# Root as a power on GpSimd, a group's sums ahead of its scores, another rule for the spare PSUM tile, and a split output tail in an attention + MLP kernel

## The chip, the cores and the metric

The kernel runs on one core of a Trainium2 chip. The metric is device time in microseconds (us), as the median of several runs. The engines are named as in the profile: PE (TensorE, matrix products), PEld (its weight loads), ACT (ScalarE), DVE (VectorE), POOL (GpSimd) and SP (SyncE, which here only issues DMAs). A q behind a name means the engine's instruction queue. [...]

## The reference

Attention with normalised queries and keys, then an MLP with a leaky rectifier:

```
batch, heads, seq, dim = 8, 12, 448, 64
q_n = q / sqrt(mean(q*q, -1) + 1e-6) * g_q           # the same for k with g_k
attn = softmax(q_n @ k_n.T / 8)                       # per batch and head
x = (attn @ v) as [8*448 tokens, 12*64]
h = x @ w_in                                          # 768 -> 2048
out = (max(h, 0) + alpha * min(h, 0)) @ w_out         # 2048 -> 768, fp32
```

All inputs and the output are fp32. Inside, the products take fp16.

## The kernel before, in words

**Tiling.** A batch has three groups of four heads, so there are 24 groups, numbered y = 3*batch + i. Partitions 0 to 63 hold two heads of the group, partitions 64 to 127 the other two. The 448 positions are cut into J = 7 tiles of 64.

**Preparing a group.** `load_qk(y)` brings q and k (tile `nat`, four DMAs), on SP, or half on ACT's queue for the first two groups. `square` makes the squares (ACT for y < 2, POOL after), `reduce` sums them on DVE (`ss`), `root` turns the 28 sums of a partition into 1/sqrt(mean + eps) (`rr`) with two ACT instructions, Ln and then Exp with scale -0.5 (L152, L153), and `scale` multiplies q and k by it (`qs`, L158), mostly on POOL. For y < 8, `turn` transposes q and k on PE (L193) into PSUM, and DVE copies them out, k with the gain g_q*g_k; later groups are transposed by DMA on SP (`turn_dma`), and `turn` is then only the product of k and gain on DVE (L179).

**Attention.** `score(y, j)` makes the transposed scores of one 64-key tile for four heads (four matmuls into the two-bank tile `sc`, of which there are two), and `soft` the exponential on ACT (L227) into `expT`. When all seven tiles of a group are there, `den(y)` sums them over the keys by 28 matmuls with ones, `log` and `invert` make the reciprocal on ACT (Ln, then Exp with scale -1, L253, L258), and `attv(y)` multiplies by v (28 matmuls), scaled by DVE into `xT` (L266). `den`, `attv` and the transposes of groups 3 to 7 share a single two-bank PSUM tile with the tag `acc`.

**MLP.** `up(b, ft)` makes 128 of the 2048 hidden columns for one batch: six matmuls (L281), an ACT copy times alpha (`ah`, L289), a DVE maximum (`gT`, L290) that frees the bank. `down(b0, t, oh)` makes 128 tokens by 384 columns of the output from a pair of batches: 16 matmuls (L298), a DVE copy (`osb`, L310), and after the second half two DMAs of 64 rows (L314). Both write to one of two single-bank PSUM tiles (tag `mm`), or, when `spare` is given, to the `acc` tile (`bank`, L271), where the trace calls them hTa and opa.

**Order.** The order on every engine is the order of the code; nothing reorders it. The attention is cut into 66 slots n of two or three score tiles (`bursts`). `dens` and `avs` say in which slot each group's `den` and `attv` stand, alternately; `turn_at`, `roots`, `prep` (before a slot), `post` (after it) and `jobs` (behind the matmuls of a `down`) say where the preparations of later groups stand. A planner deals the MLP units to the slots (`gaps`) by estimated costs, UP = 1.13, DOWN = 2.6 and a cost per slot, so that each batch's units are spread over the 15 slots or so that follow its last `attv`. A slot runs: `prep`, the first two scores and their exponentials, `den` or `attv`, the third score and its exponential, `log` and `invert`, `root` and `scale` of a later group, then the MLP units with `turn` behind the first one. The units of the last batch follow all slots (`rest`). Slots without units at the start hold dummy matmuls (`spin`) that keep PE running. In each slot without a PE transpose, the unit with number k == 2 takes the spare tile:

```
            spare = k == 2 and not turns.get(n, TD) < TD
```

The four loads of `w_in` stand together before slot 0 on POOL's queue, those of `w_out` before slots 10 to 13.

Of the kernel before, what the change touches and what calls it, by code (L numbers as in the profile page):

```python
# [9 lines left out]
FP32 = mybir.dt.float32  # L10
# [11 lines left out]
def kernel(  # L22
# [46 lines left out]
    nc.vector.memset(expb, EXP_BIAS)  # L69
    epsb = cst.tile([128, 1], FP32, name="epsb", tag="epsb")  # L70
    nc.vector.memset(epsb, RMS_EPS)
    ones = cst.tile([128, 64], FP16, name="ones", tag="ones")
    nc.vector.memset(ones, 1.0)
    ident = cst.tile([128, 128], FP16, name="ident", tag="ident")
# [40 lines left out]
    def load_w_in(c):  # L115
        nc.gpsimd.dma_start(
            out=w_in_sb[:, :, ts(c, FB)],
            in_=moe_w_in[:, ts(c, FB)].rearrange("(k p) f -> p k f", p=128),
        )
# [18 lines left out]
    def reduce(y, nm):  # L138
        if nm == "q":
            ss_t[y] = ld.tile([128, 2, 2, J], FP32, name="ss", tag="ss", bufs=4)  # L140
        nc.vector.tensor_reduce(  # L141
            out=ss_t[y][:, "qk".index(nm)].rearrange("p h j -> p (h j)").unsqueeze(2),
            in_=sqs[y, nm], axis=AXIS_X, op=ALU.add,
        )

    def root(y, nms="qk"):
        n = len(nms)
        at = "qk".index(nms[0])
        if at == 0:
            rr_t[y] = ld.tile([128, 2, 2, J], FP32, name="rr", tag="rr", bufs=4)  # L150
        rr, ss = rr_t[y][:, ds(at, n)], ss_t[y][:, ds(at, n)]
        nc.scalar.activation(out=rr, in_=ss, func=AF.Ln, scale=1.0 / D, bias=epsb[:, 0:1])  # L152
        nc.scalar.activation(out=rr, in_=rr, func=AF.Exp, scale=-0.5)  # L153

    def scale(y, nm):
        t = ld.tile([128, J, 2, D], FP16, name="qs", tag="qs", bufs=4)
        eng = nc.vector if (y, nm) in ((0, "k"), (1, "q"), (1, "k")) else nc.gpsimd
        eng.tensor_mul(  # L158
            out=t.rearrange("p j h d -> p h j d"),
            in0=nat[y, nm],  # L160
            in1=rr_t[y][:, "qk".index(nm)].unsqueeze(3).broadcast_to((128, 2, J, D)),
        )
        qs[y, nm] = t
# [11 lines left out]
    def turn(y):  # L175

        if y >= TD:
            t = qkT[y, "k"].rearrange("p j g c -> p (j g c)")
            nc.vector.tensor_scalar(  # L179
                out=t, in0=t, scalar1=gain[:, 0:1], scalar2=None, op0=ALU.mult  # L180
            )
            return
        if y < G:
            ps = [psf.tile([128, 512], FP32, name="tps", tag="mm") for _ in "qk"]
        else:
            ps2 = psa.tile([128, 2, 512], FP32, name="tps2", tag="acc")
            ps = [ps2[:, 0], ps2[:, 1]]
        tps = [
            t[:, : S].bitcast(FP16).rearrange("p (j c) -> p j c", j=J) for t in ps
        ]  # L190
        for tp, nm in zip(tps, "qk"):
            for j in range(J):
                nc.tensor.transpose(  # L193
                    tp[:, j, :], qs[y, nm][:, j].rearrange("p h d -> p (h d)"), ident
                )
        for tp, nm in zip(tps, "qk"):
            t = att.tile([128, J, 2, 64], FP16, name=f"{nm}T", tag=f"{nm}T", bufs=4)
            o = t.rearrange("p j g c -> p j (g c)")
            if nm == "q":
                nc.vector.tensor_copy(out=o, in_=tp)  # L200
            else:
                nc.vector.tensor_scalar(  # L202
                    out=o, in0=tp, scalar1=gain[:, 0:1], scalar2=None, op0=ALU.mult
                )
            qkT[y, nm] = t
# [41 lines left out]
    def den(y):  # L247
        dn = over_keys("dn", y, lambda g, par, j: ones[ds(64 * g, 64), :])
        rden[y] = dn
# [27 lines left out]
    def up(b, ft, spare=False):  # L277
        x = xT[b].rearrange("p g i c -> p (g i) c")
        hT = bank("hT", spare)
        for c in range(KM):  # L280
            nc.tensor.matmul(  # L281
                out=hT[:, :S],
                lhsT=w_in_sb[:, c, ts(ft, 128)],
                rhs=x[:, c, :],
                start=(c == 0),
                stop=(c == KM - 1),
            )
        ah = ffn.tile([128, S], FP16, name="ah", tag="ah", bufs=3)
        nc.scalar.activation(out=ah, in_=hT[:, :S], func=AF.Copy, scale=alpha_sb[:, ft : ft + 1])  # L289
        nc.vector.tensor_max(out=gT[:, ft, ds((b & 1) * S, S)], in0=hT[:, :S], in1=ah)  # L290
# [3 lines left out]
    def down(b0, t, oh, jobs=(), spare=False):  # L294

        op = bank("op", spare)
        for ft in range(NF):
            nc.tensor.matmul(  # L298
                out=op[:, :OH],
                lhsT=gT[:, ft, ts(t, 128)],  # L300
                rhs=w_out_sb[:, ft, ds(oh * OH, OH)],
                start=(ft == 0),
                stop=(ft == NF - 1),
            )
        for f, a in jobs:
            f(*a)
        if oh == 0:
            osb[b0, t] = ffn.tile([128, DM], FP32, name="osb", tag="osb", bufs=3)
        o = osb[b0, t]
        nc.vector.tensor_copy(out=o[:, ds(oh * OH, OH)], in_=op[:, :OH])  # L310
        if oh == 1:
            for half in range(2):
                bb, j = divmod(2 * t + half, J)
                nc.sync.dma_start(out=out4[b0 + bb, j], in_=o[ds(64 * half, 64)])  # L314
# [15 lines left out]
    while m < NG * J or len(avs) < NG:  # L330
        n = len(bursts)
        if len(dens) > len(avs):
            avs[n] = len(avs)
        elif len(dens) < NG and last_in.get(len(dens), n) < n:
            dens[n] = len(dens)
        wide = n in dens and dens[n] >= G or n in avs and avs[n] >= G - 1
        count = min(3 if wide else 2, NG * J - m)
        bursts.append([divmod(m + c, J) for c in range(count)])
        for y, j in bursts[n]:
            first_in.setdefault(y, n)  # L340
            if j == J - 1:
                last_in[y] = n
        m += count
# [5 lines left out]
    def at(n, f, *a):  # L349
        prep.setdefault(max(int(n), 0), []).append((f, a))  # L350
# [72 lines left out]
    rest = []  # L423
# [22 lines left out]
    for nm in "qk":  # L446
        square(0, nm)
        reduce(0, nm)
        root(0, nm)
        scale(0, nm)  # L450
    nc.vector.tensor_copy(out=cols, in_=ct[:, : NF + 2])
    nc.vector.tensor_mul(
        out=gain, in0=cols[:, NF : NF + 1], in1=cols[:, NF + 1 : NF + 2]
    )
    turn(0)
    load_v(0)
    for y in (1, 2):
# [2 lines left out]
            if y == 1:  # L460
                reduce(y, nm)
    for c in range(4):
        load_w_in(c)
        at(first - 2 + c, load_w_out, c)
    after(0, root, 1)
    for nm in "qk":
# [4 lines left out]
    for n in range(NB):  # L471
        for f, a in prep.get(n, ()):
            f(*a)
        tiles = bursts[n]
        for t in tiles[:2]:
            score(*t)
        plain = n not in dens and n not in avs
        wait = plain and gaps[n] and gaps[n][0][0] is up
        for t in tiles[:1] if wait else tiles[:2]:
            soft(*t)  # L480
        if n in dens:
            den(dens[n])
        if n in avs:
            attv(avs[n])
        for t in tiles[2:]:
            score(*t)
            soft(*t)
        late = []
        if wait:
            late = [(1, soft, t) for t in tiles[1:]]  # L490
        if n in dens:
            log(dens[n])
            if gaps[n] and gaps[n][0][0] is down:
                invert(dens[n])
            else:
                late = [(1, invert, (dens[n],))]
        if n in roots:
            y = roots[n]
            root(y)
            for nm in "qk":  # L500
                scale(y, nm)
            if y >= TD:
                turn_dma(y)
        done = 0
        for k, (f, a) in enumerate(gaps[n]):
            spare = k == 2 and not turns.get(n, TD) < TD
            if f is down:
                down(*a, jobs.pop(n, ()), spare)
            else:
                f(*a, spare)  # L510
                done += 1
                if late and done == late[0][0]:
                    for _, g, c in late:
                        g(*c)
                    late = []
            if k == 0 and n in turns:
                turn(turns[n])
        if not gaps[n] and n in turns:
            turn(turns[n])
        for _, g, c in late:  # L520
            g(*c)
        if n < first and plain and n not in turns:
            spin(4)
        for f, a in jobs.pop(n, []) + post.get(n, []):
            f(*a)
    for f, a in rest:
        f(*a)


# [28 lines left out]
```

## Time and profile before

| | us |
|---|---|
| median of 3 runs (lowest, highest) | 464.64 (464.01, 464.75) |
| the profiled execution's own time | 463.18 |
| its span, first to last instruction | 461.4 |
| PE busy | 429.8 (93%) |
| ACT busy | 290.6 (63%) |
| DVE busy | 206.8 (45%) |
| POOL busy | 170.4 (37%) |

The granted PE clock of this execution is 0.996 of full speed. "Busy" of PE counts matmuls with their latency, so 93% is not PE at its peak. A line of the timeline is: start and duration in us, engine, line of the code, operation, output<-inputs, shapes, count, and in brackets the idle time of the engine before it with what ended it. A line of the waits is: who waited for whom, the total in us, how often, and the longest. A digit in a row of slices is the busy share of one fortieth of the span, in tenths.

### The profile page before, as it was taken

What the parts mean: (1) busy time and instruction counts of PE and PEld (TensorE: products, weight loads), DVE (VectorE), ACT (ScalarE), POOL (GpSimd) and SP (SyncE); (2) the same over time, 40 slices, a digit from 0 to 9 for tenths busy, and PEclk for the clock granted to TensorE, in tenths of its full rate; (3) what the DMA queues carried; (4) which work ended last, traced back from release to release, by engine and by line L of the source; (5) the groups of instructions that cost most, each with busy time, mean ns of one, the idle gap of its engine ahead of it and who ended that gap; (6) DMA issues with size and microseconds to landing.
All of it is one profiled execution on the core that took longest, in us unless ns stands there. A gap on an engine that the chain in (4) does not pass through costs nothing.

```text
span 461.4 us, 9085 instructions
## 1 busy us (share of the span) xinstructions
PE 429.8 (93%) x3843; PEld 230.4 (50%) x3843; DVE 206.8 (45%) x297; ACT 290.6 (63%) x400; POOL 170.4 (37%) x126
## 2 busy tenths in 40 slices
PE   7877988999999999999999999999999999999995
PEld 3333444554555555545555555545555555555563
DVE  3835455453383544543463454543563324333321
ACT  4889788766785767855785766856685665322200
POOL 5759945454164156055064156055043000000000
PEclk9899999999999999999999999999999999999999
DMA  8999993764438445763438555763137311011122
GB/s 187 233 267 232 225 240 86 141 123 100 121 55 194 122 112 91 167 151 63 123 58 190 132 99 99 174 147 60 38 63 112 55 36 36 1 34 36 34 70 68
DMA packets 59849, 52.77 MB, mean 114 GB/s; under 512 B 32656, under 2 KB 56224, under 8 KB 59808
## 3 DMA queue, kind: packets, MB, share of 16 engines
q1 hardware_dynamic: 47424, 39.47, 36.3%
q0 software_dynamic: 11808, 11.81, 16.5%
q10 hardware_dynamic: 576, 0.92, 0.9%
q8 instruction: 30, 0.49, 0.5%
q14 instruction: 11, 0.09, 0.1%
HBM read 45.62 MB, written 11.01 MB: 123 GB/s over the span
## 4 chain that ended last, share of the span: by engine, by line
PE 78%; ACT 11%; DVE 8%; issue 1%; ACTq 1%; DVEq 0%
PE op L298 31%; PE hT L281 20%; PE hTa L281 7%; PE av L238 6%; PE dn L238 5%; PE sc L215 5%; ACT expT L227 5%; ACT ah L289 3%; DVE gT L290 3%; DVE ss L141 3%; PE opa L298 1%; ACT rden L253 1%; ACT rden L258 1%; PE tps L193 1%; DVE kT L202 1%
## 5 line engine op out<-in xcount | busy, mean ns | idle before, releaser
L227 ACT ACTIVATE expT<-sc,expb 128x896 f16<-128x896 f32 x168 | 159.0, 1006 | 20.2 <-PE sc L215 19.9
L298 PE MATMUL op<-w_out_sb,gT 128*128 128x384 f16 x864 | 148.0, 326 | 0.2 <-DVE gT L290 0.2
L158 POOL TENSOR_TENSOR qs<-nat,rr 128x896 f16<-128x896 f32 x45 | 77.5, 1743 | 182.6 <-issue 152.7
L289 ACT ACTIVATE ah<-hT,cols 128x448 f16<-128x448 f32 x99 | 62.8, 635 | 101.6 <-PE hT L281 101.5
L281 PE MATMUL hT<-xT,w_in_sb 128*128 128x448 f16 x594 | 125.1, 353 | 1.3 <-DVE gT L290 1.2
L298 PEld LDWEIGHTS <-gT 128*128 128x128 f16 x896 | 84.6, 98 | 65.4 <-issue 11.7
L281 PEld LDWEIGHTS <-w_in_sb 128*128 128x128 f16 x768 | 73.5, 98 | 71.3 <-issue 7.3
L290 DVE TENSOR_TENSOR gT<-hT,ah 128x448 f16<-128x448 f32 x99 | 61.8, 624 | 94.4 <-ACT ah L289 94.4
L310 DVE COPY osb<-op 128x384 f32<-128x384 f32 x54 | 30.1, 557 | 99.3 <-PE op L298 97.5
L135 POOL TENSOR_TENSOR sq<-nat 128x896 f32<-128x896 f32 x44 | 73.1, 1683 | 2.9 <-DVE kT L202 2.6
L215 PE MATMUL sc<-qT,kT 64*64 64x448 f16 x672 | 54.3, 362 | 9.2 <-ACT expT L227 5.8
L141 DVE TENSOR_REDUCE ss<-sq 128x14 f32<-128x896 f32 x48 | 49.7, 1077 | 6.5 <-ACT sq L133 6.5
L238 PE MATMUL av<-expT,vt 64*64 64x448 f16 x672 | 36.1, 350 | 6.4 <-DVE gT L290 4.4
L238 PE MATMUL dn<-expT,ones 64*64 64x448 f16 x672 | 36.1, 350 | 4.5 <-DVE gT L290 4.4
L266 DVE TENSOR_TENSOR xT<-av,rden 128x896 f16<-128x896 f32 x24 | 26.2, 1090 | 31.1 <-PE av L238 31.1
L215 PEld LDWEIGHTS <-kT 64*64 64x64 f16 x672 | 18.1, 105 | 39.3 <-issue 29.3
L281 PE MATMUL hTa<-xT,w_in_sb 128*128 128x448 f16 x174 | 37.6, 352 | 0.0
L238 PEld LDWEIGHTS <-vt 64*64 64x64 f16 x672 | 21.1, 107 | 18.8 <-issue 9.0
L238 PEld LDWEIGHTS <-ones 64*64 64x64 f16 x672 | 21.5, 107 | 15.9 <-issue 6.4
L289 ACT ACTIVATE ah<-hTa,cols 128x448 f16<-128x448 f32 x29 | 18.4, 635 | 13.2 <-PE hTa L281 13.2
L290 DVE TENSOR_TENSOR gT<-hTa,ah 128x448 f16<-128x448 f32 x29 | 18.1, 625 | 12.1 <-ACT ah L289 11.9
L258 ACT ACTIVATE rden<-rden 128x896 f32<-128x896 f32 x24 | 23.0, 957 | 0.6
(36 smaller groups left out, 128.5 us busy)
## 6 DMA issues: line engine op xcount, KB each, us to landing
out_dram<-osb SPq DMA_DIRECT2D x56, 192.0 KB, 2.7
nat<-in_q_dram SPq DMA_DIRECT2D x46, 224.0 KB, 4.8
nat<-in_k_dram SPq DMA_DIRECT2D x46, 224.0 KB, 6.5
vt<-in_v_dram POOLq DMA_DIRECT2D x16, 336.0 KB, 8.0
w_in_sb<-in_moe_w_in_dram POOLq DMA_DIRECT2D x4, 768.0 KB, 20.1
w_out_sb<-in_moe_w_out_dram POOLq DMA_DIRECT2D x4, 768.0 KB, 15.2
nat<-in_q_dram ACTq DMA_DIRECT2D x2, 224.0 KB, 4.6
nat<-in_k_dram ACTq DMA_DIRECT2D x2, 224.0 KB, 6.0
```

The source lines that it names most:

```text
L135: nc.gpsimd.tensor_mul(out=sqf, in0=src, in1=src)
L141: nc.vector.tensor_reduce(out=ss_t[y][:, "qk".index(nm)].rearrange("p h j -> p (h j)").unsqueeze(2), in_=sqs[y, nm], axis=AXIS_X, op=ALU.add,)
L158: eng.tensor_mul(out=t.rearrange("p j h d -> p h j d"), in0=nat[y, nm], in1=rr_t[y][:, "qk".index(nm)].unsqueeze(3).broadcast_to((128, 2, ...
L215: nc.tensor.matmul(out=sc[ds(64 * g, 64), par, :S].rearrange("p (j c) -> p j c", j=J), lhsT=kT[ds(64 * par, 64), j, g, :], rhs=qT[ds(64 * ...
L227: nc.scalar.activation(out=expT[y][:, j], in_=scs[y, j][:, :, :S], func=AF.Exp, scale=QK_SCALE, bias=expb[:, 0:1],)
L238: nc.tensor.matmul(out=acc[ds(64 * par, 64), g, :S], lhsT=weights(g, par, j), rhs=e[ds(64 * g, 64), j, par, :], start=(j == 0), stop=(j == ...
L258: nc.scalar.activation(out=r, in_=r, func=AF.Exp, scale=-1.0)
L281: nc.tensor.matmul(out=hT[:, :S], lhsT=w_in_sb[:, c, ts(ft, 128)], rhs=x[:, c, :], start=(c == 0), stop=(c == KM - 1),)
L289: nc.scalar.activation(out=ah, in_=hT[:, :S], func=AF.Copy, scale=alpha_sb[:, ft : ft + 1])
L290: nc.vector.tensor_max(out=gT[:, ft, ds((b & 1) * S, S)], in0=hT[:, :S], in1=ah)
L298: nc.tensor.matmul(out=op[:, :OH], lhsT=gT[:, ft, ts(t, 128)], rhs=w_out_sb[:, ft, ds(oh * OH, OH)], start=(ft == 0), stop=(ft == NF - 1),)
L310: nc.vector.tensor_copy(out=o[:, ds(oh * OH, OH)], in_=op[:, :OH])
```

## The change

- `root` for y >= 1 runs on POOL: one operation for sum/64 + eps and one for the power -0.5, with a constant tile of exponents. Group 0 stays on ACT.
- `scale(1, "k")` goes from DVE to POOL; for group 0 the copy of the transposed q goes from DVE to ACT; `cols` and `gain` are made before the root of k of group 0 and no longer after its scaling.
- `up` takes its six chunks of `xT` in an order in which both chunks of the batch's last group come last.
- In the slots of `den(2)` and `attv(2)`, these stand before the scores (`lead`), `den(2)` with `log` and `invert` right behind it.
- The slot of `attv(2)` has two score tiles and no longer three, so that most later slots begin one tile earlier in the sequence, and the planner deals units, transposes and loads to the slots anew. The number of slots stays at 66. One slot, 19 (`den(5)`), then has no unit.
- The loads of `w_in` stand before slots 0, 1, 3 and 4.
- The unit in the spare tile is the first, but never the last one of its gap, before which 2.3 us (in a `den` slot), 1.2 (`attv`) or 0.1 of the planner's unit costs have passed.
- In `rest`, every third unit takes the spare tile.
- The last 128 rows of the output are copied and sent in parts: the first 384 columns as soon as they are made, the other 384 in two halves, one by DVE and SP, one by ACT and its queue.

```diff
     def root(y, nms="qk"):
...
+        if y:
+            nc.gpsimd.tensor_scalar(
+                out=rr, in0=ss, scalar1=1.0 / D, scalar2=RMS_EPS,
+                op0=ALU.mult, op1=ALU.add,
+            )
+            nc.gpsimd.tensor_tensor(
+                out=rr, in0=rr, in1=power, op=ALU.pow
+            )
+            return
         nc.scalar.activation(out=rr, in_=ss, func=AF.Ln, scale=1.0 / D, bias=epsb[:, 0:1])
         nc.scalar.activation(out=rr, in_=rr, func=AF.Exp, scale=-0.5)
...
-        eng = nc.vector if (y, nm) in ((0, "k"), (1, "q"), (1, "k")) else nc.gpsimd
+        eng = nc.vector if (y, nm) in ((0, "k"), (1, "q")) else nc.gpsimd
...
-            if nm == "q":
+            if nm == "q" and y == 0:
+                nc.scalar.copy(out=o, in_=tp)
+            elif nm == "q":
                 nc.vector.tensor_copy(out=o, in_=tp)
...
     def up(b, ft, spare=False):
...
-        for c in range(KM):
+        order = [g * G + i for i in range(G) for g in range(2)]
+        for c in order:
...
     def down(b0, t, oh, jobs=(), spare=False):
...
+        if (b0, t) == (B - 2, J - 1):
+            rows2 = out4[B - 1, ds(J - 2, 2)]
+            n = oh + 1
+            for h in range(n):
+                at = ds(oh * OH + h * (OH // n), OH // n)
+                piece = ds(h * (OH // n), OH // n)
+                if h:
+                    nc.scalar.copy(out=o[:, at], in_=op[:, piece])
+                else:
+                    nc.vector.tensor_copy(out=o[:, at], in_=op[:, piece])
+                (nc.scalar if h else nc.sync).dma_start(
+                    out=rows2[:, :, at], in_=o[:, at]
+                )
+            return
...
-        wide = n in dens and dens[n] >= G or n in avs and avs[n] >= G - 1
+        wide = n in dens and dens[n] >= G or n in avs and avs[n] >= G
...
         reduce(0, nm)
+        if nm == "k":
+            nc.vector.tensor_copy(out=cols, in_=ct[:, : NF + 2])
+            nc.vector.tensor_mul(
+                out=gain, in0=cols[:, NF : NF + 1], in1=cols[:, NF + 1 : NF + 2]
+            )
         root(0, nm)
         scale(0, nm)
...
     for c in range(4):
-        load_w_in(c)
+        at(c + c // 2, load_w_in, c)
         at(first - 2 + c, load_w_out, c)
...
+        lead = n in (den_at[G - 1], av_at[G - 1])
+        if lead and n in dens:
+            den(dens[n])
+            log(dens[n])
+            invert(dens[n])
+        elif lead:
+            attv(avs[n])
         for t in tiles[:2]:
             score(*t)
...
+        spare_at, clock = None, 0.0
+        for k, (f, a) in enumerate(gaps[n][:-1]):
+            free = 2.3 if n in dens else 1.2 if n in avs else 0.1
+            if spare_at is None and clock >= free and not turns.get(n, TD) < TD:
+                spare_at = k
+            clock += DOWN if f is down else UP
         for k, (f, a) in enumerate(gaps[n]):
-            spare = k == 2 and not turns.get(n, TD) < TD
+            spare = k == spare_at
...
-    for f, a in rest:
-        f(*a)
+    for k, (f, a) in enumerate(rest):
+        f(*a, spare=k % 3 == 2)
```

More of the change, by code (lines that the diff above doesn't have):

```diff
@@ L71 @@
     nc.vector.memset(epsb, RMS_EPS)
+    power = cst.tile([128, 2, 2, J], FP32, name="power", tag="power")
+    nc.vector.memset(power, -0.5)
     ones = cst.tile([128, 64], FP16, name="ones", tag="ones")
@@ L284, in up @@
                 rhs=x[:, c, :],
-                start=(c == 0),
-                stop=(c == KM - 1),
+                start=(c == order[0]),
+                stop=(c == order[-1]),
             )
@@ L448 @@
         reduce(0, nm)
+        if nm == "k":
[3 more added lines that the diff above has]
+            )
         root(0, nm)
         scale(0, nm)
[L451 to L454, printed above, removed]
     turn(0)
@@ L480 @@
             soft(*t)
-        if n in dens:
+        if n in dens and not lead:
             den(dens[n])
-        if n in avs:
+        if n in avs and not lead:
             attv(avs[n])
@@ L490 @@
             late = [(1, soft, t) for t in tiles[1:]]
-        if n in dens:
+        if n in dens and not lead:
             log(dens[n])
```

## The prediction

> **What bounds the kernel now.** I read the page first: its slices show three stages.
>
> ```profile
> span 461.4 us, 9085 instructions
> ...
> PE   7877988999999999999999999999999999999995
> ...
> ACT  4889788766785767855785766856685665322200
> POOL 5759945454164156055064156055043000000000
> ```
>
> A slice is 11.5 us. For the first four or so ACT is nearly full and PE is not; then PE is at 9 to the end, and ACT and POOL have room. The windows confirm it: from 13.6 to 47.6 us (first exponential to first matmul of the MLP) ACT is busy 30.70 of 34.00 us; from 91.1 to 400 us PE is busy 299.81 of 308.90. So a saving on ACT counts before 48 us only, and after that only PE's own waits count. The timeline at the start, ACT and POOL:
>
> ```profile
> 15.57 1.68 POOL L135 TENSOR_TENSOR sq<-nat 128x896 f32<-128x896 f32 x1 [0.32 <-DVE ss L141]
> 17.19 3.38 POOL L116 DMA_DIRECT2D w_in_sb<-in_moe_w_in_dram  x4
> 20.54 3.41 POOL L135 TENSOR_TENSOR sq<-nat 128x896 f32<-128x896 f32 x2
> 23.91 3.34 POOL L158 TENSOR_TENSOR qs<-nat,rr 128x896 f16<-128x896 f32 x2
> ...
> 22.56 0.32 ACT L152 ACTIVATE rr<-ss,epsb 128x28 f32<-128x28 f32 x1 [0.47 <-DVE ss L141]
> ...
> 31.66 0.32 ACT L152 ACTIVATE rr<-ss,epsb 128x28 f32<-128x28 f32 x1 [1.20 <-DVE ss L141]
> ```
>
> A root on ACT costs two instructions (0.54 us) and, twice or three times, a wait for the row sums in front of queued exponentials. POOL runs without a break from 15.57 to 27.25, and the transposes of group 2 start at 27.24: POOL ends that wait. Next, PE's waits, and the place where one falls:
>
> ```profile
> PE dn L238 <- DVE gT L290: 4.4, 5, 0.9
> PE av L238 <- DVE gT L290: 4.4, 5, 0.9
> ```
>
> ```profile
> 164.76 1.30 PE L281 MATMUL hTa<-xT,w_in_sb 128*128 128x448 f16 x6
> 165.99 0.57 PE L215 MATMUL sc<-qT,kT 64*64 64x448 f16 x8
> 167.44 1.52 PE L238 MATMUL dn<-expT,ones 64*64 64x448 f16 x28 [0.88 <-DVE gT L290]
> ```
>
> hTa is an up unit in the two-bank accumulator tile (L273). Being the last unit of its gap, it still holds the tile when the next sums want it: ACT copy 0.63, DVE maximum 0.62 and two hand-overs must pass, and only 0.57 us of scores cover them. Ten such waits of 0.88 are 8.8 us. Last, the tail, timeline of PE and then of the end:
>
> ```profile
> 404.68 2.43 PE L281 MATMUL hT<-xT,w_in_sb 128*128 128x448 f16 x12
> 407.35 1.29 PE L281 MATMUL hT<-xT,w_in_sb 128*128 128x448 f16 x6 [0.24 <-DVE gT L290]
> ...
> 456.67 0.56 DVE L310 COPY osb<-op 128x384 f32<-128x384 f32 x1 [2.04 <-PE op L298]
> 457.26 1.10 SPq L314 DMA_DIRECT2D out_dram<-osb  x2
> ```
>
> Twelve matmuls at the 0.189 us between starts end their issue at 406.95; the next starts at 407.35: 0.40 lost, because two banks serve three up units in a row. It happens six times.
>
> [...]
>
> **The change, part by part.**
>
> *Power on Pool, groups 1 to 23.* Off ACT: 23 x 0.54 = 12.4 us, worth time only before 48 us. On POOL: a scalar operation and a power over 28 elements a partition. Unknown price. From below 0.1 us each (POOL's small memsets take 0.10). [...] I take R = 1.5 us for both with their hand-overs, keeping 0.3 to 4.7. Later groups hide it: group 8's kT lands at 102.1 and its product starts at 111.4; the least such spare time I find is 5.7 us (group 10), and POOL then has 6.7 us of work in some 14.
>
> At the start it is not hidden. In the built order POOL's queue holds, ahead of root 1: both squares of group 2 (end 17.25, their loads land at 13.41 and 15.41) and one w_in issue (0.85), so root 1 starts at 18.1, against 15.84 on ACT. Then R, 0.1 hand-over, and scale(1,k), now on POOL, 1.69 (DVE does q alongside, 1.1): 19.9 + R. Seven transposes, hand-overs and one score: 0.9. The transposes precede the score of tile (0,6) on PE, so its exponential goes from 20.19 to 20.8 + R = 22.3: +2.1. Root 2's 0.97 leaves ACT (22.56 with 0.47 of wait, to 23.05): +1.15. Then POOL: w_in 0.85, squares 3.36, w_in 0.85, R, 0.1, scales 3.36: group 2 scaled at 28.4 + 2R = 31.4, before at 27.25. The exponential of (1,5), behind these transposes, goes from 28.56 to 32.4: +3.8. Root 3 with its wait gives back 1.67: +2.15 at (2,0). DVE's reductions of group 3 come after these copies, so root 3 ends at about 36.2 and scaling at 39.6, just before its transposes are due at 40: hidden. SP's loads of groups 4 and 5 start 2.5 to 4 us later, since they wait for the scales; POOL reaches their squares at about 40: hidden. The w_in issues at slots 0, 1, 3, 4 delay the last chunk's issue to about 32; its column is used past 70 us.
>
> *First group.* gain and cols move into DVE's wait for root 0, q's copy goes to ACT (about 0.9 in place of the square that follows): kT 0.65 earlier, but the squares of group 1 then hold ACT: first exponential 14.04 to 13.7, -0.35. It is inside the slack of the next steps, so 0 in the sum.
>
> *Third group ahead, narrower bursts.* den(2), its logarithm and inverse before the scores of slot 11, attv(2) before those of slot 12. ACT saves root 4 (1.0 us), but waits about 1.4 us for den(2), which a spin of 0.93 precedes on PE. Before, the first hT starts at 47.63; now the two exponentials (3,1) and (3,2) end at 48.9, two scores follow, hT at 49.4: +1.8. Three up units in a row there wait 0.5 for a bank. Slot 14 starts 1.4 late with one tile of scores less done (0.3): **+1.7**. The new order of the six chunks lets a first up unit begin before xT's third part; the scores already cover that: 0.
>
> *Gaps dealt anew to slab 0.* The planner gives slot 18 both down units and slot 19 none. There three exponentials (2.9), the logarithm (0.92) and the tile's release stand against 2.9 us of PE work; then the inverse delays the next exponential: PE idles about 2.2. The transposes of group 6 come after a down unit, saving one of the 1.12 waits for xT (at 78.53), and an osb wait of 0.15 goes: **+0.9**.
>
> *Spare rule.* The unit in the accumulator tile is never last: **-8.8**, and -0.2 of small ones. But some gaps lose it: slot 24 has four up units without one, 25 three, 34 and 49 two ups and a down, 64 three and a down. In a sums slot ACT does three exponentials and a logarithm (to 4.4 us after its start) before it copies the first unit; the bank is free at 5.8, PE wants it at 4.7: 1.1 each in slots 34 and 49, 1.5 in 24 (the inverse delays the second copy too), 0.5 in 25, 0.4 in 64: **+4.6**.
>
> *Tail.* Every third unit in the accumulator tile: -6 x 0.40 = **-2.4**. Output in parts: the last copy is 192 wide (DVE's 557 ns at 384 and 624 at 448 suggest some 0.36, -0.2), and one issue per queue instead of two in turn (second at +0.51), landing 2.7 as before: **-0.65**.
>
> Sum: 1.7 + 0.9 - 9.0 + 4.6 - 2.4 - 0.65 = -4.85. The profiled execution took 463.18 us around its span of 461.4, which becomes 456.5; the runs' median is 464.64, 1.5 above that execution, so the forecast is 464.64 - 4.85 = 459.8 us. Differences under 0.2% (0.9 us) can't be told from no change.
>
> **Rivals.** *A slow power (slower).* R enters the start twice, before transposes 1 and 2. From R = 3.9 the gain is gone (-4.85 + 2 x 2.4); at 4.7 it is +1.5, and the third use then shows as well, for root 3's scaling no longer ends before its transposes: some 467 to 471. For it: no price, and POOL without a pause in the trace. Against it: 28 elements only.
> *No new bank waits (faster still).* If ACT is ahead in those slots, since roots no longer stand before the copies, the 4.6 does not come and slot 19 costs half: 464.64 - 10.5 = 454. For it: ACT at 68% in the middle stage. Against it: the exponentials precede the copies in ACT's order anyhow.
> *The start swallows it (no change).* PE waits of 2 and 3 us before transposes 1 and 2 could bring a spell of half clock (the trace has one, 14.0 to 17.4) and the late start could carry into slots 14 to 18, where ACT is nearly full: +4 more, 464.
>
> **Numbers.** Likeliest case 0.47 (own range 456.5 to 463); no new waits 0.18; start swallows it 0.08; slow power 0.27, part of it only to 466. Faster: 0.47 + 0.18, less a little for the first case's upper end: 0.64; same 0.08; slower 0.28. Range for 8 in 10: from 453, in the second case, to 468, well into the first rival.
>
> **What would show it.** The POOL row of the power: its ns; first hT near 49.4; den and av waits on gT gone; waits of hT or op on gT near slots 24, 34, 49 (about 120, 185, 285 us); one long PE wait near 90 us in slot 19; none in the tail. I am wrong if the power takes over 3.9 us, if the start is not late, or if den still waits for gT.

## The result, and the profile after

The changed kernel takes 486.67 us, median of 4 runs (484.36 to 488.28), against 464.32 for the kernel before (4 runs, 463.79 to 464.75). The ratio is 1.0478, with a 95% interval of 1.0429 to 1.0527. It is slower by 22.35 us where a gain of 4.85 was forecast, and it lies outside the range of 453 to 468.

The page of the kernel after, whose profiled execution took 487.64 us; slices are now 12.15 us wide:

```profile
span 485.9 us, 9116 instructions
...
PE   7377687989999999799999999799999999999991
...
POOL 5897999989939991917996774647966000000000
PEclk9867999999999999989999999899999999999997
```

POOL, which was at 6 or less after its first five slices, is at 9 for long stretches. PE has dips in slices 2 to 5, again at slices 17 and 26, and the granted PE clock falls in these slices or the next. The trace's clock records show it at half of full speed ("half clock" below) for 10.2 us from 21.8 us on, for 6.8 from 38.9, and for 3.4 each from 83.2, 206.1 and 311.9. The groups of instructions (busy us in all, mean ns of one; then idle time before them and who ended it) say what fills POOL:

```profile
L159 POOL TENSOR_TENSOR rr<-rr,power 128x28 f32<-128x28 f32 x23 | 110.6, 4807 | 1.9
...
L190 DVE TENSOR_SCALAR kT<-kT,gain 128x896 f16<-128x896 f16 x16 | 24.8, 1550 | 0.0
```

One power takes 4.81 us, so a root on POOL takes some 5.1 with its scalar operation and hand-overs (17.90 to 23.02 us for group 1). The second line is a surprise. This DVE product was not touched by the change. Before, it stood on the page so:

```profile
L179 DVE TENSOR_SCALAR kT<-kT,gain 128x896 f16<-128x896 f16 x16 | 9.7, 604 | 0.0
```

Four spots of the two profiled executions cut the difference of the spans into stretches (each by the spots' times in both traces; of matmuls the start counts):

| stretch | before | after | difference | forecast |
|---|---|---|---|---|
| start to first hT | 47.6 | 60.4 | +12.8 | +1.7 |
| first hT to last av | 354.2 | 362.8 | +8.6 | +0.9 - 9.0 + 4.6 = -3.5 |
| last av to last matmul | 54.5 | 52.1 | -2.4 | -2.4 |
| last matmul to end | 5.1 | 10.6 | +5.5 | -0.65 |

So three of four stretches went wrong. The timeline of the start, kernel after:

```profile
17.90 0.21 POOL L155 TENSOR_SCALAR rr<-ss 128x28 f32<-128x28 f32 x1
18.19 4.83 POOL L159 TENSOR_TENSOR rr<-rr,power 128x28 f32<-128x28 f32 x1
23.10 2.60 POOL L169 TENSOR_TENSOR qs<-nat,rr 128x896 f16<-128x896 f32 x1
24.21 0.93 PE L204 MATMUL tps<-ident,qs 128*128 128x128 f16 x7 [6.31 <-DVE qs L169]
...
27.25 1.91 ACT L240 ACTIVATE expT<-sc,expb 128x896 f16<-128x896 f32 x2 [8.00 <-PE sc L228]
```

PE waits 6.31 us for the first scaled q, then ACT waits 8.00 us for scores. ACT, which bounded this stage at 30.70 of 34.00 us busy, now has 18.22 us of work there (windows, 13.6 to 47.6 us; the columns are the length, then the busy us and the count of PE, PEld, DVE, ACT and POOL, the granted clock, the busy share of the 16 DMA engines, and GB/s):

```profile
13.60:47.60 34.00, 21.07 (x212) 9.72 (x208) 10.43 (x12) 18.22 (x20) 30.24 (x17) 0.75 1.02 195
```

The second dip of PE, timeline of the kernel after:

```profile
201.36 1.39 POOL L112 DMA_DIRECT2D vt<-in_v_dram  x2
201.74 4.62 DVE L190 TENSOR_SCALAR kT<-kT,gain 128x896 f16<-128x896 f16 x1
202.75 3.34 POOL L137 TENSOR_TENSOR sq<-nat 128x896 f32<-128x896 f32 x2
206.41 0.96 PE L228 MATMUL sc<-qT,kT 64*64 64x448 f16 x8 [2.91 <-DVE kT L190]
207.16 2.66 PE L251 MATMUL dn<-expT,ones 64*64 64x448 f16 x28
```

The product takes 4.62 us and ends 0.27 us after POOL's run of v's descriptors and squares (at 206.09). PE waits 2.91 us for it, and the 28 matmuls behind it take 2.66 us where the kernel before needs 1.52: PE has fallen to half clock for 3.4 us. The same picture stands at 307.54 us. Last, the waits of the kernel after:

```profile
PE sc L228 <- DVE kT L190: 7.0, 3, 2.9
...
PE hT L295 <- DVE gT L304: 2.3, 6, 0.8
PE op L312 <- DVE gT L304: 1.5, 2, 0.7
PE dn L251 <- DVE gT L304: 0.2, 1, 0.2
```

Den and attv have all but ceased to wait for gT (8.8 us before); a wait for kT of 7.0 us has come in.

### The profile page after: what moved, and what is told of

It reads as the page before. It is cut to its first block, busy times and chain, and to the rows that moved or that the text cites. A ratio compares the mean times of both kernels' runs of the same rounds, so it can differ in the third digit from the quotient of the medians.

```text
span 485.9 us, 9116 instructions
## 1 busy us (share of the span) xinstructions
PE 435.9 (90%) x3843; PEld 232.2 (48%) x3843; DVE 219.2 (45%) x296; ACT 281.4 (58%) x356; POOL 287.6 (59%) x173
## 3 DMA queue, kind: packets, MB, share of 16 engines
q10 hardware_dynamic: 706, 1.02, 0.8%
## 4 chain that ended last, share of the span: by engine, by line
PE 72%; POOL 12%; ACT 6%; DVE 5%; issue 3%; ACTq 1%; POOLq 0%
PE op L312 29%; PE hT L295 16%; PE hTa L295 8%; PE sc L228 6%; PE dn L251 5%; POOL rr L159 5%; PE av L251 5%; POOL sq L137 3%; DVE kT L190 2%; POOL qs L169 2%; ACT expT L240 2%; PE opa L312 2%; ACT ah L303 1%; DVE gT L304 1%; DVE ss L143 1%
## 5 line engine op out<-in xcount | busy, mean ns | idle before, releaser
L312 PE MATMUL op<-w_out_sb,gT 128*128 128x384 f16 x848 | 145.9, 326 | 1.5 <-DVE gT L304 1.5
L295 PE MATMUL hT<-xT,w_in_sb 128*128 128x448 f16 x558 | 118.3, 355 | 2.4 <-DVE gT L304 2.3
L159 POOL TENSOR_TENSOR rr<-rr,power 128x28 f32<-128x28 f32 x23 | 110.6, 4807 | 1.9
L295 PEld LDWEIGHTS <-w_in_sb 128*128 128x128 f16 x768 | 73.9, 98 | 74.0 <-issue 10.2
L303 ACT ACTIVATE ah<-hT,cols 128x448 f16<-128x448 f32 x93 | 59.2, 636 | 66.8 <-PE hT L295 66.8
L304 DVE TENSOR_TENSOR gT<-hT,ah 128x448 f16<-128x448 f32 x93 | 58.0, 624 | 79.6 <-ACT ah L303 79.6
L339 DVE COPY osb<-op 128x384 f32<-128x384 f32 x51 | 28.4, 558 | 85.4 <-PE op L312 85.4
L303 ACT ACTIVATE ah<-hTa,cols 128x448 f16<-128x448 f32 x35 | 22.2, 634 | 53.6 <-PE hTa L295 53.6
L155 POOL TENSOR_SCALAR rr<-ss 128x28 f32<-128x28 f32 x23 | 4.9, 213 | 78.2 <-DVE ss L143 77.5
L295 PE MATMUL hTa<-xT,w_in_sb 128*128 128x448 f16 x210 | 45.4, 352 | 0.0
L251 PE MATMUL dn<-expT,ones 64*64 64x448 f16 x672 | 40.2, 380 | 0.2 <-DVE gT L304 0.2
L304 DVE TENSOR_TENSOR gT<-hTa,ah 128x448 f16<-128x448 f32 x35 | 21.8, 622 | 26.2 <-ACT ah L303 26.2
## 6 DMA issues: line engine op xcount, KB each, us to landing
out_dram<-osb SPq DMA_DIRECT2D x55, 192.0 KB, 2.7
w_out_sb<-in_moe_w_out_dram POOLq DMA_DIRECT2D x4, 768.0 KB, 10.6
```

Source lines behind the costliest of these rows:

```text
L159: nc.gpsimd.tensor_tensor(out=rr, in0=rr, in1=power, op=ALU.pow)
L251: nc.tensor.matmul(out=acc[ds(64 * par, 64), g, :S], lhsT=weights(g, par, j), rhs=e[ds(64 * g, 64), j, par, :], start=(j == 0), stop=(j == ...
L295: nc.tensor.matmul(out=hT[:, :S], lhsT=w_in_sb[:, c, ts(ft, 128)], rhs=x[:, c, :], start=(c == order[0]), stop=(c == order[-1]),)
L312: nc.tensor.matmul(out=op[:, :OH], lhsT=gT[:, ft, ts(t, 128)], rhs=w_out_sb[:, ft, ds(oh * OH, OH)], start=(ft == 0), stop=(ft == NF - 1),)
```

## The experiments

Each kernel is compared with runs of the kernel before on the same chip, and differences are to those (463.48 to 463.67).

**The power taken out.** Everything of the change stays but the root.

```diff
-        if y:
...
-            nc.gpsimd.tensor_tensor(
-                out=rr, in0=rr, in1=power, op=ALU.pow
-            )
-            return
```

> The changed kernel with the roots of groups 1 to 23 back on ACT, all else as changed. Theory (the power, 4.8 us each, makes the late start, and through POOL's lateness also the waits of scores for kT near 206 and 312 us): first hT back to 47-50 us from 60.4, no wait for kT over 1.2 us, den and av waits on gT still gone; left over are the slow output at the end (+5.5) and the gains of the spare tile, so 456 to 462 us. Rival (the other order of slots and loads makes them): the start stays at least 6 us late and the kT waits stay, 470 us or more.

Measured: 461.81 us (19 runs, 460.34 to 463.46), ratio 0.9964 (0.9953 to 0.9974), -1.86 us. So the power is worth 22.35 + 1.86 = 24.2 us, more than the whole loss. The product of kT and gain is back to at most 0.97 us. The new waits for banks show undisturbed here (waits, this kernel):

```profile
PE hT L284 <- DVE gT L293: 3.0, 6, 0.9
PE op L301 <- DVE gT L293: 2.0, 2, 1.0
```

**The power alone**, put into the kernel before.

```diff
+        if y:
...
+            nc.gpsimd.tensor_tensor(
+                out=rr, in0=rr, in1=power, op=ALU.pow
+            )
+            return
```

> The kernel before with only the root of groups 1 to 23 as a power on POOL. Theory (power): first hT 8 to 13 us late, and kT waits of some us where DVE's product of kT and gain meets POOL's work: 474 to 486 us. Rival (the order of slots is needed for the loss): under 470 us.

Measured: 497.15 us (496.83 to 502.0), ratio 1.0748 (1.0698 to 1.0798), +33.5 us: worse than expected and than in the changed kernel. The first hT starts at 64.6 us, 17.0 later than before, and the stretch from there to the last av is 16.7 us longer. Here all four w_in issues stand ahead of root 1 on POOL, which starts at 19.91 us; the changed kernel has one issue there and starts root 1 at 17.90. What else makes its start the better one was not tried. The wait of scores for kT is there again, 7.7 us in this kernel.

**The output tail made whole again** in the changed kernel, **and split alone** in the kernel before.

```diff
-        if (b0, t) == (B - 2, J - 1):
-            rows2 = out4[B - 1, ds(J - 2, 2)]
...
-                (nc.scalar if h else nc.sync).dma_start(
-                    out=rows2[:, :, at], in_=o[:, at]
-                )
-            return
```

> The changed kernel with the last rows of the output copied and sent as before. Theory (the DMAs of the split tail, whose outermost dimension is 2, use few of the 16 engines: 47 GB/s and 9.5 us from the last copy to the end, against 4.2 before): the end follows the last matmul by 4.8 us again, 480.5 to 482 us. Rival (the end is late for what lies before it): 486 us and over.

> The kernel before with only the split output tail. Theory (few DMA engines): +5 to +6 us, 469 to 471 us. Rival (the split itself saves its 0.65 us, as the prediction had it): 463 to 464.5 us.

Measured: whole 479.51 us (477.63 to 479.7), +15.84, so the split costs 6.5 there, a little more than expected; split alone 469.0 us (468.75 to 469.35), ratio 1.0117 (1.0102 to 1.0132), +5.33. The end of the split kernel, timeline; ACTq is a DMA issue:

```profile
457.52 0.32 ACT L318 COPY osb<-op 128x192 f32<-128x192 f32 x1 [20.97 <-DVE osb L320]
457.87 1.12 ACTq L321 DMA_DIRECT2D out_dram<-osb  x1
```

The compute ends at 457.84, the span at 467.4. How fast the bytes go in that time the windows show (last two columns); first the kernel before, then the split alone:

```profile
457.20:461.40 4.20, 0.00 (x0) 0.00 (x0) 0.03 (x1) 0.00 (x0) 0.00 (x0) 0.97 0.36 94
```

```profile
457.20:467.40 10.20, 0.00 (x0) 0.00 (x0) 0.29 (x1) 0.32 (x1) 0.00 (x0) 0.66 0.11 36
```

The last 128 rows, 384 KB, need 10 us at 36 GB/s, with 0.11 of the 16 DMA engines busy, which is 1.8 of them. (The 47 GB/s of the expectation is not what the windows give; in the changed kernel it is 33, from 473.6 us to the end.) The form of the access was the suspect: `rows2[:, :, at]` has 2 blocks of 64 tokens as its outermost dimension.

**The split with 64-row DMAs**, in the kernel before.

```diff
-                (nc.scalar if h else nc.sync).dma_start(
-                    out=rows2[:, :, at], in_=o[:, at]
-                )
+                for half in range(2):
+                    (nc.scalar if h else nc.sync).dma_start(
+                        out=out4[B - 1, J - 2 + half, :, at], in_=o[ds(64 * half, 64), at]
+                    )
```

> The kernel before with the split output tail, each part sent as two DMAs of 64 rows and not as one whose outermost dimension is 2. Theory[...]: no loss left, and up to the predicted gain of 0.65 us: 463.0 to 463.8 us. Rival (short runs of 768 and 1536 bytes or two queues are slow): 467 us and over.

Measured: 463.37 us (13 runs, 462.88 to 464.16), ratio 0.9998 (0.999 to 1.0006), -0.11 us. The 5.3 us are gone with three more issues and no other edit, so the outermost dimension of 2 was the cause. The gain of 0.65 isn't seen either; the interval leaves room for a gain of 0.46 at most.

**The spare rule alone**, slots and `rest`, in the kernel before.

```diff
-            spare = k == 2 and not turns.get(n, TD) < TD
+            spare = k == spare_at
...
-    for f, a in rest:
-        f(*a)
+    for k, (f, a) in enumerate(rest):
+        f(*a, spare=k % 3 == 2)
```

> The kernel before with only the other rule for the spare tile in the slots and every third unit of the tail in it. Theory (the ten 0.88 us waits and the six of the tail go, few new bank waits since the old dealing has four ups without a spare only in slot 24): -8.8 - 2.4 + 1 to 1.5, so 453 to 455 us. Rival (the waits only move to the banks): 459 us or more.

Measured: 453.12 us (452.66 to 453.79), ratio 0.977 (0.9754 to 0.9787), -10.53. Its waits:

```profile
PE hT L281 <- DVE gT L290: 2.3, 6, 1.0
```

The waits of dn and av are gone, and few new ones have come: one of 1.02 us at 124.4 us, the others 0.25 each. The stretch from the first hT to the last av is 8.1 us shorter than before, the one behind it 2.4. This part is worth more than the forecast gave to the whole change.

**Change without power and without the split tail.**

```diff
-        if y:
...
-            nc.gpsimd.tensor_tensor(
-                out=rr, in0=rr, in1=power, op=ALU.pow
-            )
-            return
...
-        if (b0, t) == (B - 2, J - 1):
...
```

> The changed kernel with roots on ACT and the output's end as before: what is left of the change without the two parts held for the loss. If the parts add up, 461.8 less the 5.3 that the split tail cost alone, or less the 7.2 that it gave back in the changed kernel: 454.5 to 456.5 us. If slot order and new bank waits had cost what the spare tile brings: 460 us or more.

Measured: 456.66 us (456.38 to 458.43), ratio 0.9853 (0.9831 to 0.9876), -6.99. Against the spare rule alone, what is left (the lead, the two-tile slot and the new deal) costs 3.5 us. Waits of hT and op on gT are 5.0 us here, 2.5 with the spare rule alone, which is most of it. That is a sum over one execution each, not a run of its own.

**The product of kT and gain on ACT**, in the changed kernel. Rival readings of the dips were a late kT from POOL's queue, which this edit leaves, and a DVE that is held, which it takes away.

```diff
-            nc.vector.tensor_scalar(
-                out=t, in0=t, scalar1=gain[:, 0:1], scalar2=None, op0=ALU.mult
-            )
+            nc.scalar.activation(out=t, in_=t, func=AF.Copy, scale=gain[:, 0:1])
```

> The changed kernel with the product of kT and gain of groups 8 to 23 on ACT and not on DVE (about 0.9 us each there). Theory (DVE's product cannot run while POOL works on squares, scales or a load's descriptors, so that scores wait, and PE falls to half clock after the two longest waits): waits of scores for kT under 1 us, no half clock near 206 and 312 us, 7 to 13 us faster than the changed kernel, 473 to 480 us. Rival (the transposes land late, whoever multiplies): 485 us and over, same waits.

Measured: 476.35 us (475.04 to 476.9), ratio 1.0264 (1.024 to 1.0289), 9.65 us better than the changed kernel. From first hT to last av it takes 349.3 us (62.5 to 411.9), 4.8 less than the kernel before and as long as in both kernels without the power (349.3). The tile kT in both kernels (ns, lowest/median/highest; first and last start), first after, then this one:

```profile
L190 DVE TENSOR_SCALAR kT<-kT,gain x16: 442/1377/4620, 131.9 to 391.2; 128x896 f16<-128x896 f16 x16
```

```profile
L190 ACT ACTIVATE kT<-kT,gain x16: 1032/1052/1058, 128.2 to 377.9; 128x896 f16<-128x896 f16 x16
```

On ACT it takes 1.05 us each time, and no score waits for it. That kT arrives late was not the matter; that DVE holds it was. The half-clock spells near 206 and 312 us are gone too.

The first exponentials of the groups, against those of the kernel without power and split tail, show where the time goes. The changed kernel is 11.9 us late at group 3 (54.0 against 42.2 us), 16.1 at group 5, and still 16.1 at group 7; then it loses 1.0 at group 8, 4.2 at groups 12 and 13, and 4.3 at groups 18 and 19, where the three waits for kT stand. With the product on ACT the lateness is 14.3 us at group 5 and 14.1 at the last group. So the product costs 9.3 us in the trace, and all else about the power is paid by group 5.

**Price of the power.** In the kernel before, powers and products of constant tiles on POOL ahead of `rest`, used nowhere.

```diff
+    for w in (1, 7, 14, 28, 56, 112, 224):
+        nc.gpsimd.tensor_tensor(out=po[:, :w], in0=pz[:, :w], in1=pw[:, :w], op=ALU.pow)
+        nc.gpsimd.tensor_tensor(out=po[:, :w], in0=pz[:, :w], in1=pw[:, :w], op=ALU.mult)
+    for p in (16, 64):
+        nc.gpsimd.tensor_tensor(out=po[:p, :28], in0=pz[:p, :28], in1=pw[:p, :28], op=ALU.pow)
```

> The kernel before, and at the end of its slots, where POOL has nothing to do, powers and products of constant tiles on POOL, 128 x 1, 7, 14, 28, 56, 112 and 224 wide, and powers of 28 on 16 and on 64 partitions; their results are used nowhere. If the power costs by the element: 4.8 us at 28, near 0.2 + 0.165 us per element, so 1.4 at 7, 9.4 at 56, 37 at 224, and the same on 16 partitions as on 128[...]. If it is a fixed cost (a call or a load of code): near 4.8 us at every width. Time as before, 463 to 466 us.

Measured: 465.12 us, one run. The groups by shape (L533 is the product, L535 the power on fewer partitions):

```profile
L532 POOL TENSOR_TENSOR po<-pz,pw 128x224 f32<-128x224 f32 x1 | 36.1, 36114 | 0.1
...
L535 POOL TENSOR_TENSOR po<-pz,pw 16x28 f32<-16x28 f32 x1 | 4.8, 4787 | 0.1
...
L532 POOL TENSOR_TENSOR po<-pz,pw 128x1 f32<-128x1 f32 x1 | 0.6, 577 | 0.1
...
L533 POOL TENSOR_TENSOR po<-pz,pw 128x28 f32<-128x28 f32 x1 | 0.2, 243 | 0.1
```

From 1 to 224 elements the time grows by 35.54 us, 0.159 us for each element, on top of 0.42. At 28 elements that is 20 times the product. Sixteen partitions take as long as 128 (4.79 and 4.80 us), so packing the sums on fewer partitions can only lengthen it.

**The power from group 5 on**, in the changed kernel: the first four groups' roots, whose transposes wait for POOL at the start, go back to ACT.

```diff
-        if y:
+        if y > 4:
```

> The changed kernel with the power only from group 5 on; groups 1 to 4, which the first slots wait for, take their roots from ACT. Theory (the loss at the start is the power's time ahead of the transposes of groups 1 and 2, and the later kT waits are a loss of their own): first hT at 48.5 to 50 us, the waits of scores for kT still some 6 to 8 us with their half clock, 11 to 13 us faster than the changed kernel, 473 to 476 us. Rival (one delay carried through: POOL lags since the start): the kT waits go as well, 465 us or less.

Measured: 468.86 us (467.74 to 470.11), ratio 1.0117 (1.0095 to 1.0138), +5.38; better than was expected. The first hT starts at 46.5 us. So the powers of groups 1 to 4 cost 22.35 - 5.38 = 17.0 us, those of groups 5 to 23 5.38 + 1.86 = 7.2 us. The wait for kT stays in full:

```profile
PE sc L228 <- DVE kT L190: 6.9, 3, 2.9
```

Of its two long waits only the second, at 292.2 us, goes with half clock. The first does not, and its 28 sums take the usual 1.52 us:

```profile
187.74 0.57 PE L228 MATMUL sc<-qT,kT 64*64 64x448 f16 x8 [2.91 <-DVE kT L190]
188.27 1.52 PE L251 MATMUL dn<-expT,ones 64*64 64x448 f16 x28
```

**The lead alone**, on top of the spare rule.

```diff
+        lead = n in (den_at[G - 1], av_at[G - 1])
+        if lead and n in dens:
+            den(dens[n])
+            log(dens[n])
+            invert(dens[n])
+        elif lead:
+            attv(avs[n])
         for t in tiles[:2]:
             score(*t)
```

> The kernel before with the rule for the spare tile and the tail's third units, and with den(2) and attv(2) ahead of the scores of their slots. The prediction's step (ACT waits for den(2), two exponentials come later): 0.5 to 1.5 us slower than with the rule alone, 453.6 to 454.6 us. Rival (the sums come earlier, so the MLP starts earlier): 452.5 us or less.

Measured: 453.92 us (452.94 to 454.91), ratio 0.9794 (0.9774 to 0.9813), -9.56. The lead costs about 1.0 us; the intervals of the two ratios overlap, so its size is loose. First hT goes from 48.2 to 49.9 us.

**A version out of what helps**: the kernel before with the spare rule, where a `den` slot's unit may take the spare tile after 2.2 us of unit costs instead of 2.3, and the split tail by 64 rows.

```diff
+            free = 2.2 if n in dens else 1.2 if n in avs else 0.1
```

> The kernel before with the rule for the spare tile at 2.2 in place of 2.3 in slots of sums, so that the third of four ups in slot 24 gets the tile, every third unit of the tail in it, and the split output tail sent as DMAs of 64 rows. Theory: 453.1 as with the rule alone, less 1.0 for slot 24 and 0.5 for the tail, 451.4 to 452.4 us. Rival (slot 24 only hands its wait on, the tail gives nothing): 453 us and over.

Measured: 451.84 us (451.68 to 452.72), ratio 0.9753 (0.9738 to 0.9767), -11.64: faster than both kernels. The 2.2 gives the unit after two ups (2 x 1.13 = 2.26) the spare tile, so a `den` slot of four units or more that begins with two ups has it again. Its waits for banks:

```profile
PE hT L281 <- DVE gT L290: 1.2, 5, 0.2
```

They are 1.2 us where the spare rule of the change had 2.3: the wait of 1.02 us at 124.4 us is gone, and -11.64 against -10.53 is in line with that, though from two batches. That the kernel before also has 1.2 is chance, for there it is five of the six waits in the tail.

## Why the prediction was wrong

**Step that failed first: "I take R = 1.5 us".** The root takes 5.1. Of the range that the step kept, 0.3 to 4.7, only the lower end had a measured number behind it, POOL's memsets of 0.10 us; the 1.5 and the upper end were the author's estimates with no row for them, and the measured root lies above both. The start's own formula nearly holds with 5.1: group 2 scaled at 28.4 + 2 x 5.1 = 38.6 (measured 39.35), exponential of (0,6) at 20.8 + 5.1 = 25.9 (27.25). So the mechanism was right and the size was off; the size is 2 x 3.6 = 7.2 of the +12.8. With it alone the prediction's sum gives 467.0 us, so it is 7.2 of the 27.2 us between forecast and result. (One reading under this step was loose: before, the transposes of group 2 start at 27.24 us with no idle time of PE, so POOL's end at 27.25 ended no wait there.)

The other 3.9 us of the start over the forecast's +1.7 was in no term of the sum; the rival "a slow power" had named one part, root 3, whose scaling ends at 51.66 us, with a PE wait of 0.96 for it. Also seen there are transposes at half clock (0.93 us for seven against 0.56 later) after PE's wait of 6.31, and POOL's scaling of k at 2.60 us beside DVE's of q, where 1.69 was reckoned. A rival had listed the half clock for a shorter wait. The spell from 21.8 us lasts 10.2 us, three times the 3.4 of each spell after the start; the one from 38.9 us, after PE waits of 2.56 and 1.08, lasts 6.8, two times. How the 3.9 divides was not tried. Nor is the start known to better than some 3 us: without the power it was at 49.7 us in one kernel and, with powers from group 5 on, at 46.5 in the other, with 0.90 and 1.00 of granted clock from 13.6 to 47.6 us.

**Step that failed second: "Later groups hide it".** They do from group 6 on: with the product on ACT, the power costs nothing from there to the end. Groups 4 and 5, called hidden too, were not. PE waits 1.08, 0.71 and 1.09 us for POOL's scalings of them (67.68, 80.83 and 82.48 us) and 1.58 for v (77.17 us), half clock follows from 83.2, and group 5 is 4.2 us further back than group 3. And the step only asked whether kT would be late. The late POOL pushes v's descriptors and squares onto DVE's product, and DVE then holds until they end. Predicted cost 0, measured 9.65 us by moving the product. It divides into the waits of 7.0 us on kT and half clock behind the two longest: (2.66 - 1.52) us in the 28 sums, each time, 9.3 in all.

The hold was there before the change, only short. Of the 16 products of the changed kernel nine start beside a scaling or a square, and each ends 0.25 us after that operation; here the second scaling ends at 253.11 us and the product at 253.35 (timeline):

```profile
249.77 3.34 POOL L169 TENSOR_TENSOR qs<-nat,rr 128x896 f16<-128x896 f32 x2
...
251.55 1.80 DVE L190 TENSOR_SCALAR kT<-kT,gain 128x896 f16<-128x896 f16 x1
```

In the kernel before, 12 of 16 do the same and take up to 0.97 us, since they start late in a scaling; that is why the mean stands at 604 ns and the shortest at 443. The two of 4.62 us start during the first of v's two descriptor issues and are held through four POOL instructions. Not everything is held: the product that reads PSUM (L215) takes 0.68 us beside squares too (52.87 us), as it does elsewhere, and the three products beside the power take 0.44 us, as they do alone. Why DVE holds is not shown; shown is that the product is slow on DVE beside POOL's scalings, squares and descriptors (up to 4.62 us), and not on ACT (1.06 at most), and that the long holds come only with the power on POOL (up to 0.97 us with the roots back on ACT).

**Step that failed third: "landing 2.7 as before".** The landing of 2.7 us belonged to DMAs whose outermost dimension is 64 rows; the new ones have 2. Predicted -0.65, measured +5.3 alone and +5.1 to +6.5 in the change. The windows show the split alone at 36 GB/s with 1.8 of the 16 DMA engines busy, and the kernel before at 94 with 5.8 (0.36 of 16). DMAs of 64 rows undo it: the span ends 3.8 us after the last copy (457.94 to 461.7), and 9.6 us after it where the outermost dimension is 2 (457.84 to 467.4). By what mechanism the access form does this was not shown. The prediction counted issues and took the duration from another access form.

**What held.** The tail: -2.4 in both traces. The spare rule: dn and av waits gone, -8.8. With -0.2 and -2.4 less 2.5 of new waits the terms give -8.9, the run -10.5; where the 1.6 more come from is open. The new waits for banks: 4.6 predicted, 5.0 in the kernel without the power, 0.7 of it at the start (51.7 us) and the rest near the slots that were named (0.85 at 121.9, 0.77 at 129.7, 1.02 at 192.0 and 293.6 us). The lead was put at +1.7 with the rest of the start; alone it costs 1.0. In the emptied slot 19 of the changed kernel PE idles 1.6 us where 2.2 were predicted, in four pieces of 0.31 to 0.52 us (106.7 to 110.3 us) and not in one wait.

**The rival "a slow power"** named the right first cause, and had 467 to 471 us for it; the product and the store were not in it. The terms as measured bring it to the result: 459.8 as forecast, +7.2 for the root at the start, +3.9 for the rest of the start, +9.65 for the product, +6.15 for the end (5.5 + 0.65), in sum 486.7, against 486.67. That it meets so closely is luck: the terms come from single executions and other batches, the spans of the two traces differ by 24.5 us and not by 22.35, and the 4.2 us lost between group 3 and group 5 stand in no term.

## What to carry to other kernels

An operation that no row of the trace shows has to be measured by itself before work is moved to it, and until then the price of the slow case is the one to plan with: it enters a start once for every group whose preparation nothing covers. An engine that is made busier costs not only by being late; look also for the instructions of other engines that slow down while it runs (here DVE's product, 0.44 us alone and 4.62 beside POOL's descriptors and squares). The form of a DMA's access belongs to its price as much as its bytes do (here the same 384 KB at 36 GB/s with an outermost dimension of 2, at 94 with 64 rows).

## What the runs showed that was not expected

- A power on POOL takes 0.42 us and 0.159 us for each element of a partition, as long on 16 partitions as on 128; a product of 28 elements takes 0.24.
- DVE's fp16 product of an SBUF tile and a column takes 0.44 us alone. Beside a scaling or square of POOL it ends 0.25 us after that operation; started in POOL's run of descriptors and squares, it takes 4.62. During the power itself it wasn't slowed: 0.44 at 146.4, 221.1 and 326.9 us.
- A PE wait of 2.9 us can bring a spell of half clock of 3.4 us (at 206 and 312 us here, at 292 with the power from group 5 on), but need not: none came at 187.7 us in that last kernel.
- The last 384 KB of the output, sent by three DMAs whose outermost dimension is 2, move at 36 GB/s; by two DMAs of 64 rows, at 94.
